# Attention with beacon keys and a two-layer MLP: pair 0's q by GpSimd's casting DMA, k first on SyncE's queue, four probability buffers

## The chip, the cores and the metric

The kernel runs on one core of one Trainium2 chip. The core has five engines with an instruction queue each: TensorE (PE, matmuls and transposes), ScalarE (ACT), VectorE (DVE), GpSimd (POOL) and SyncE (SP, which here only issues DMAs). Times are device microseconds of one execution; ten executions of the kernel before have a median of 351.33 us (350.22 to 353.68).

## The reference

For 8 batches and 8 heads, 576 queries of width 64 attend causally to 576 keys, and besides to 16 beacon keys that every query sees. The results of the heads are put side by side, and a two-layer MLP with a leaky ReLU follows on all 4608 rows.

```
k_all = concat([beacon_k, k]); v_all = concat([beacon_v, v])
a = softmax(where(causal, -1e9, q @ k_all.T / sqrt(64)))     # beacons never masked
x = (a @ v_all) -> rows (batch, query), columns (head, 64)   # 4608 x 512
h = x @ w_in                                                 # 512 x 2048
out = maximum(0.01 * h, h) @ w_out                           # 2048 x 512
```

## The kernel before

Work goes by *pairs* of heads, numbered g = 0 to 31: four pairs to a batch, two pairs to a *group* of `load_qk` (one load brings two pairs of one tensor, in two DMAs of q and two of k, one for each pair `e`). A matmul's 128 partitions hold the two heads of a pair.

For a pair, the steps are these. `t_q` transposes q (which = 0) or k (which = 1) on PE, 18 small transposes each into a PSUM tile `tp`, and DVE copies them in order into `qT` or into `kT`; from pair 8 on, a DMA transpose on SP (`turn_pairs`) and two GpSimd copies (`in_order`) do this instead. `beacon_columns` puts the 16 beacon keys into the first columns of `kT`. `score(g, n)`, n = 0 to 3, makes four blocks of transposed scores, and ACT takes the exponential of each block out of PSUM into the pair's probabilities `aT`. There are two PSUM buffers for scores, so block n + 2 waits for the exponential of block n. `masks_by_tri` (DVE, pairs 0 and 1) or `masks` (GpSimd, four instructions) clears what is above the diagonal. `value(g, 0)` and `value(g, 1)` multiply the probabilities with v, whose last column is one, so that the row sums come along; DVE takes the reciprocal and scales. `finish(g)` transposes the result on PE, and DVE copies it into `xT`, the MLP's operand.

The MLP goes in chunks of 512 rows. `fill()` issues the next *group* of four matmuls of 512 columns: `moe1` (first layer, followed by ACT's leaky ReLU) or `moe2` (a quarter of a second-layer tile). The first group needs `finish(3)`, that is all four pairs of batch 0, and the first half of `w_in`. These groups are the filling between the attention steps for the rest of the kernel.

Nothing is planned by a scheduler: `tc.manual_schedule` (L489) keeps each engine's instructions in the order in which the program writes them, and `tc` puts semaphore waits where data or buffers need them. The order by pairs is the loop of L573: pairs 0 to 4 in one branch (L577), pairs 5, 6 and 7 with a branch each, pair 8 and on in the general part. `keep_busy(n)` (L477) issues n small matmuls of the identity that compute nothing.

In the start (L499 to L522) the first pair goes its own way: `load_first_pair` (L141) loads q on SP and k on ACT in float32 into a borrowed `v_raw` tile, ACT and DVE cast them to bf16 (L510 to L512), and `t_q(0, 0)` and `t_q(0, 1)` follow on PE. All other q and k come by GpSimd's DMA, which casts on the way. `load_v(b, after)` issues v in six DMAs on SP, the first of which waits for another DMA. `cast_v` on GpSimd makes bf16 pieces of it. GpSimd's queue carries, in one order, its DMA issues, v casts, masks and beacon columns; a wait of one of them holds all that is behind it.

Buffers that matter: three `a_bufs` for probabilities (pair g has buffer g % 3, so pair 3's exponentials wait for value(0)), three `k_bufs`, three pairs of raw q and k tiles (`qkpool`), two PSUM buffers for scores and four (`ps_one`) for everything else.

## Time and profile before

| what | us |
|---|---|
| median of ten executions | 351.33 |
| the profiled execution | 350.98 |
| its span, first to last instruction | 349.3 |
| PE busy | 340.2 |
| ACT busy | 187.4 |
| POOL busy | 197.0 |
| DVE busy | 98.1 |
| PE's first scores start | 8.35 |
| first exponential starts | 8.78 |
| first MLP group starts | 28.75 |

Times within the span are counted from its first instruction. A line of the order of time shows start, duration, engine, source line, operation, tiles, shapes and how many instructions are merged in it; in square brackets stands how long the engine was idle before it, and what ended that. "SPq" and "POOLq" are the queues that issue DMAs. The share of a DMA queue is the time its packets took as a share of the core's 16 DMA engines; it can exceed 100%, as packets overlap.

### The profile page before, as it was taken

What the parts mean: (1) busy time and instruction counts of PE and PEld (TensorE: products, weight loads), DVE (VectorE), ACT (ScalarE), POOL (GpSimd) and SP (SyncE); (2) the same over time, 40 slices, a digit from 0 to 9 for tenths busy, and PEclk for the clock granted to TensorE, in tenths of its full rate; (3) what the DMA queues carried; (4) which work ended last, traced back from release to release, by engine and by line L of the source; (5) the groups of instructions that cost most, each with busy time, mean ns of one, the idle gap of its engine ahead of it and who ended that gap; (6) DMA issues with size and microseconds to landing.
All of it is one profiled execution on the core that took longest, in us unless ns stands there. A gap on an engine that the chain in (4) does not pass through costs nothing.

```text
span 349.3 us, 7405 instructions
## 1 busy us (share of the span) xinstructions
PE 340.2 (97%) x3045; PEld 172.8 (49%) x3045; DVE 98.1 (28%) x240; ACT 187.4 (54%) x277; POOL 197.0 (56%) x335
## 2 busy tenths in 40 slices
PE   8889999999999999999999999999999999999996
PEld 7564654334554444444544444455444554444444
DVE  3694530113342222222321223222321331000121
ACT  3987846665356863486347833684368304633300
POOL 7595837597999799767977779667321100000000
PEclk9999999999999999999999999999999999999999
DMA  8999999958969895992489319970110011000012
GB/s 163 193 157 202 176 212 180 201 111 164 236 147 135 158 151 108 186 191 49 82 181 186 88 34 190 185 124 31 52 41 0 2 76 46 0 30 32 30 60 92
DMA packets 85121, 40.88 MB, mean 117 GB/s; under 512 B 69040, under 2 KB 79280, under 8 KB 85088
## 3 DMA queue, kind: packets, MB, share of 16 engines
q1 hardware_dynamic: 72544, 26.52, 36.6%
q0 software_dynamic: 12128, 13.54, 24.9%
q10 hardware_dynamic: 416, 0.36, 0.5%
q8 instruction: 24, 0.39, 0.4%
q14 instruction: 9, 0.07, 0.1%
HBM read 37.22 MB, written 9.44 MB: 134 GB/s over the span
## 4 chain that ended last, share of the span: by engine, by line
PE 79%; DMA 11%; POOL 3%; SPq 3%; DVE 2%; issue 1%; ACT 0%; POOLq 0%
PE acc L444 36%; PE acc L422 28%; PE av L386 6%; PE sc L306 6%; DMA v_raw<-in_v_dram 4%; DMA q_raw<-in_q_dram 3%; SPq L218 2%; DMA q_turn<-q_nat 1%; DMA v_raw<-in_k_dram 1%; PE tp L408 1%; DVE osb L453 1%; DMA k_raw<-in_k_dram 1%; POOL aT L355 1%; DVE xT L413 1%; POOL v_aug L227 1%
## 5 line engine op out<-in xcount | busy, mean ns | idle before, releaser
L422 PE MATMUL acc<-xT,w_in_sb 128*128 128x512 bf16 x576 | 139.3, 379 | 1.4 <-DVE xT L413 1.4
L315 ACT ACTIVATE aT<-sc 128x1024 bf16<-128x1024 f32 (+3 forms) x128 | 103.8, 870 | 66.2 <-PE sc L306 60.7
L444 PE MATMUL acc<-w_out_sb,gT 128*128 128x512 bf16 (+1 forms) x592 | 139.0, 374 | 0.0
L429 ACT ACTIVATE gT<-acc 128x512 bf16<-128x512 f32 x144 | 85.7, 601 | 73.8 <-PE acc L422 73.6
L444 PEld LDWEIGHTS <-gT 128*128 128x128 bf16 x592 | 53.1, 98 | 58.5 <-issue 6.1
L422 PEld LDWEIGHTS <-w_in_sb 128*128 128x128 bf16 x576 | 51.8, 98 | 59.3 <-issue 4.6
L453 DVE COPY osb<-acc 128x512 f32<-128x512 f32 (+1 forms) x37 | 25.1, 677 | 127.8 <-PE acc L444 127.5
L355 POOL TENSOR_SCALAR_AFFINE_SELECT aT<-aT 128x224 bf16<-128x224 bf16 (+1 forms) x120 | 48.7, 447 | 18.7 <-PE av L386 9.9
L286 POOL COPY qT<-q_turn 128x576 bf16<-128x576 bf16 x24 | 28.6, 1194 | 40.0 <-PE sc L306 23.9
L386 PEld LDWEIGHTS <-aT 128*128 128x128 bf16 (+1 forms) x960 | 36.9, 98 | 15.6 <-issue 2.5
L386 PE MATMUL av<-v_aug,aT 128*128 128x65 bf16 (+1 forms) x960 | 40.1, 194 | 0.7 <-POOL v_aug L227 0.4
L306 PE MATMUL sc<-qT,kT 64*128 64x80 bf16 (+4 forms) x384 | 35.8, 283 | 2.4 <-ACT aT L315 1.5
L396 DVE TENSOR_TENSOR x_nat<-av,rec 128x384 bf16<-128x384 f32 x64 | 31.4, 491 | 2.2
L286 POOL COPY kT<-k_turn 128x576 bf16<-128x576 bf16 x24 | 28.5, 1186 | 0.8 <-DMA k_turn<-k_nat 0.8
L413 DVE COPY xT<-tp 128x576 bf16<-128x576 bf16 x32 | 14.5, 453 | 45.4 <-PE tp L408 45.4
L395 DVE RECIPROCAL rec<-av 128x6 f32<-128x6 f32 x64 | 11.9, 186 | 53.0 <-PE av L386 52.9
L306 PEld LDWEIGHTS <-kT 64*128 64x128 bf16 x384 | 12.3, 94 | 27.9 <-issue 16.2
L227 POOL CAST v_aug<-v_raw 128x512 bf16<-128x512 f32 (+1 forms) x35 | 20.8, 635 | 6.4 <-DMA v_raw<-in_v_dram 6.2
L133 POOL DMA_DIRECT2D q_raw<-in_q_dram x31 | 19.6, 632 | 4.5 <-DMA w_out_sb<-in_moe_w_out_dram 4.3
L133 POOL DMA_DIRECT2D k_raw<-in_k_dram x31 | 19.6, 633 | 3.5 <-DMA w_out_sb<-in_moe_w_out_dram 2.4
L408 PEld LDWEIGHTS <-x_nat 128*128 128x128 bf16 (+2 forms) x160 | 11.1, 97 | 6.7 <-DVE rec L395 0.2
L167 POOL COPY q_nat<-q_raw 128x1152 bf16<-128x1152 bf16 x12 | 13.9, 1156 | 0.3 <-DMA q_raw<-in_q_dram 0.3
(43 smaller groups left out, 94.3 us busy)
## 6 DMA issues: line engine op xcount, KB each, us to landing
out_dram<-osb SPq DMA_DIRECT2D x35, 256.0 KB, 2.4
v_raw<-in_v_dram SPq DMA_DIRECT2D x24, 256.0 KB, 5.0
q_raw<-in_q_dram POOLq DMA_DIRECT2D x31, 144.0 KB, 5.6
k_raw<-in_k_dram POOLq DMA_DIRECT2D x31, 144.0 KB, 6.1
w_in_sb<-in_moe_w_in_dram POOLq DMA_DIRECT2D x2, 1024.0 KB, 9.2
w_out_sb<-in_moe_w_out_dram POOLq DMA_DIRECT2D x2, 1024.0 KB, 12.4
v_raw<-in_v_dram SPq DMA_DIRECT2D x8, 224.0 KB, 3.8
v_raw<-in_v_dram SPq DMA_DIRECT2D x8, 160.0 KB, 4.4
```

The source lines that it names most:

```text
L133: dma = nc.gpsimd.dma_start(out=dst[e * RP : (e + 1) * RP], in_=src[b, h0 : h0 + 2].rearrange("h (p i) d -> p h i d", i=RI),)
L227: eng.tensor_copy(out=dst[0 : ROWS[c], c, :, 0:D], in_=t[0 : ROWS[c], c])
L286: nc.gpsimd.tensor_copy(out=dst.rearrange("c (p i) -> c p i", i=RI), in_=t[:, :, e].rearrange("c i p -> c p i"),)
L306: nc.tensor.matmul(out=sc[:, par, col - c0 : col - c0 + w], lhsT=kT[ps_, c * 128 : (c + 1) * 128], rhs=qT[ps_, q0 : q0 + w], start=True, s ...
L315: nc.scalar.activation(out=aT[:, :, c0 : c0 + w], in_=sc[:, :, 0:w], func=AF.Exp, scale=0.125)
L355: nc.gpsimd.affine_select(out=part, in_=part, compare_op=ALU.is_ge, fill=0.0, base=base, channel_multiplier=-1, pattern=pattern,)
L386: nc.tensor.matmul(out=avv[:, n, 0 : D + 1], lhsT=aT[0 : ROWS[c], par, a0 : a0 + 128], rhs=va[0 : ROWS[c], c, 2 * hp + par, :], start=(c = ...
L396: nc.vector.tensor_tensor(out=x_nat[:, t0:t1].rearrange("p t e d -> p (t e) d"), in0=avv[:, :, 0:D], in1=rec[:, n0:n1, None].to_broadcast( ...
L422: nc.tensor.matmul(out=acc, lhsT=w_in_sb[:, j, fc * 128 : (fc + 1) * 128], rhs=xT[:, j, i * 512 : (i + 1) * 512], start=(j == 0), stop=(j ...
L429: nc.scalar.activation(out=gT[i][:, fc, :], in_=acc, func=AF.Prelu, alpha=0.01)
L444: nc.tensor.matmul(out=acc[:, 0:w], lhsT=gT[i][:, fc, t * 128 : (t + 1) * 128], rhs=w_out_sb[:, fc, c0 : c0 + w], start=(fc == 0), stop=(f ...
L453: nc.vector.tensor_copy(out=osb[:, 0:w], in_=acc[:, 0:w])
```

## The change

Pair 0's q now comes by GpSimd's casting DMA straight to bf16 in its ordinary `q_raw` tile, issued right behind the identity and ahead of the other six q and k loads. k, still in float32, is the first DMA on SP's queue. Only k is cast, one head by ACT and one by DVE. k's transposes come before q's, and each of the two PSUM results is copied in halves by two engines (`copy_part`). The number of `keep_busy` matmuls before the first scores goes from 24 + 18 + 4 + 3 to 24 + 11 + 1 + 4. v(0) waits for pair 1's q.

There are four `a_bufs`, and two instead of three pairs of raw q and k tiles. The order of the early pairs is written anew: value(0,1) moves behind the third scores block of pair 3, value(1) and finish(0) into pair 3, value(2) and finish(1) into pair 4, value(3) and finish(2) into pair 5. In pair 5 the transposes for pair 6 come ahead of finish(3) and of the first MLP group. value(4) moves from pair 6 into pair 7, behind all scores of pair 7 and two MLP groups. Batch 1's four q and k loads of group 0 are issued together before v's second piece is cast, and `w_in`'s first half is issued before v's last two pieces are cast. In pair 7, `masks(7)` comes ahead of `load_qk(2, 0)`. Before pair 8's scores 31 instead of 30 MLP groups are done.

```diff
-    qkpool = ctx.enter_context(tc.tile_pool(name="qkpool", bufs=3))
+    qkpool = ctx.enter_context(tc.tile_pool(name="qkpool", bufs=2))
...
-    a_bufs = [singles.tile([128, 2, ACOLS], BF16, name=f"aT{i}") for i in range(3)]
+    a_bufs = [singles.tile([128, 2, ACOLS], BF16, name=f"aT{i}") for i in range(4)]
...
     def load_first_pair():
         load_beacon_k(0, 2, nc.scalar)
...
-        for eng, src, dst in zip((nc.sync, nc.scalar), (q, k), first_raw):
-            last = eng.dma_start(out=dst, in_=src[0, 0:2].rearrange("h (p i) d -> p h i d", i=RI))
-        return last
+        load_qk(0, 0, ())
+        q_rows, k_rows = qk_rows(0, 0, 0)
+        nc.sync.dma_start(out=first_k[0], in_=k_rows)
+        make_identity(nc, ident)
+        nc.gpsimd.dma_start(out=qk_raw[0, 0][0][0:RP], in_=q_rows)
...
-        parts = 2 if g == 0 and which == 1 else 1
-        for part in range(parts):
+
+        def copy_part(part, copy):
             p = slice(part * RP // parts, (part + 1) * RP // parts)
             copy(
...
+        return copy_part
+
+    def transpose_pair(g):
+        for which in range(2):
+            t_q(g, which)(0, nc.vector.tensor_copy)
...
-            probs[g] = a_bufs[g % 3]
+            probs[g] = a_bufs[g % 4]
...
-        first = load_first_pair()
-        make_identity(nc, ident)
-        load_qk(0, 0)
+        load_first_pair()
+        load_v(0, after=load_qk(0, 0, (1,))[0])
         load_qk(0, 1)
-        load_v(0, after=first)
...
         keep_busy(24)
         beacon_transposes(0, 2)
+        nc.scalar.copy(out=first_cast[:, 0], in_=first_k[0][:, 0])
+        nc.vector.tensor_copy(out=first_cast[:, 1], in_=first_k[0][:, 1])
         beacon_columns(0, nc.vector)
+        keep_busy(11)
+        copy_k = t_q(0, 1, 2)
+        copy_k(0, nc.scalar.copy)
+        keep_busy(1)
+        copy_q = t_q(0, 0, 2)
+        copy_q(0, nc.vector.tensor_copy)
+        copy_q(1, nc.scalar.copy)
+        copy_k(1, nc.vector.tensor_copy)
+        keep_busy(4)
         beacon_columns(1, nc.vector)
-        nc.vector.tensor_copy(out=first_cast[0], in_=first_raw[0])
-        nc.scalar.copy(out=first_cast[1][:, 0], in_=first_raw[1][:, 0])
-        nc.vector.tensor_copy(out=first_cast[1][:, 1], in_=first_raw[1][:, 1])
-        keep_busy(18)
-        t_q(0, 0)
-        keep_busy(4)
-        t_q(0, 1, nc.scalar.copy)
-        keep_busy(3)
...
-        cast_v(0, nc.gpsimd, 0, 1)
-        load_qk(1, 0, (0,))
...
             if g == 1:
+                cast_v(0, nc.gpsimd, 0, 1)
+                load_v(1, after=load_qk(1, 0)[-1])
                 beacon_columns(3, nc.gpsimd)
                 cast_v(0, nc.gpsimd, 1, 3)
-                load_v(1, after=load_qk(1, 0, (1,)))
+                load_w_in(0)
                 cast_v(0, nc.gpsimd, 3, 5)
-                load_w_in(0)
...
+            if g == 3:
+                score(3, 0)
+                score(3, 1)
+                transpose_pair(4)
+                score(3, 2)
+                value(0, 1)
+                score(3, 3)
+                masks(3)
+                value(1, 0)
+                value(1, 1)
+                finish(0)
+                continue
+
+            if g == 4:
+                score(4, 0)
+                score(4, 1)
+                transpose_pair(5)
+                value(2, 0)
+                score(4, 2)
+                value(2, 1)
+                finish(1)
+                score(4, 3)
+                masks(4)
+                continue
+
             if g == 5:
                 score(5, 0)
+                value(3, 0)
+                score(5, 1)
                 value(3, 1)
-                score(5, 1)
                 finish(2)
                 score(5, 2)
-                finish(3)
-                fill()
                 score(5, 3)
                 masks(5)
-                fill()
-                t_q(6, 0)
-                t_q(6, 1)
+                transpose_pair(6)
+                finish(3)
                 fill()
                 fill()
...
             if g == 7:
                 score(7, 0)
                 score(7, 1)
+                fill()
+                fill()
+                score(7, 2)
+                score(7, 3)
+                masks(7)
+                load_qk(2, 0)
+                value(4, 0)
+                value(4, 1)
                 value(5, 0)
                 finish(4)
                 value(5, 1)
-                score(7, 2)
-                score(7, 3)
-                load_qk(2, 0)
-                masks(7)
+                value(6, 0)
                 finish(5)
...
-                while done1[0] + done2[0] < 30:
+                while done1[0] + done2[0] < 31:
                     fill()
```

## The prediction

> **What bounds the kernel now.** I read the busy shares, then the stretches by stage, then TensorE's (PE's) waits, then the order of time.
>
> ```profile
> span 349.3 us, 7405 instructions
> PE 340.2 (97%) x3045; PEld 172.8 (49%) x3045; DVE 98.1 (28%) x240; ACT 187.4 (54%) x277; POOL 197.0 (56%) x335
> ```
>
> PE is busy 340.2 of 349.3 us, so at most 9.1 us can be had without removing matmuls, and nothing removes any but fillers. Stretches, cut at the first scores (8.35), at pair 3's scores (18.79), at the first MoE group (28.75) and at pair 8's scores; columns are width, PE, weight loads, DVE, ACT, POOL, clock, DMA share, GB/s:
>
> ```profile
> 0.00:8.35 8.35, 6.69 (x89) 6.04 (x89) 3.15 (x16) 2.82 (x5) 6.16 (x17) 1.00 0.83 161
> 8.35:18.79 10.44, 9.13 (x202) 6.01 (x203) 7.13 (x14) 9.64 (x13) 6.29 (x11) 1.00 1.14 192
> 18.79:28.75 9.96, 9.12 (x218) 6.67 (x215) 8.79 (x22) 8.07 (x10) 8.51 (x22) 1.00 1.00 164
> 28.75:66.00 37.25, 36.53 (x376) 18.91 (x374) 10.83 (x28) 24.54 (x40) 24.12 (x38) 1.00 1.14 191
> 66.00:346.00 280.00, 278.58 (x2172) 135.14 (x2169) 67.76 (x161) 142.36 (x212) 151.97 (x249) 1.00 0.52 102
> ```
>
> After 66 us PE loses 1.4 us in 280: the change touches nothing there but the number of probability buffers. Before 28.75 PE is not the bound. Up to 18.79 ACT's exponentials are (9.64 of 10.44; PE's time contains 28 filler matmuls); then DVE is nearly full (8.79 of 9.96). The same in ACT's and PE's order of time:
>
> ```profile
> 6.07 0.67 ACT L511 CAST k_nat<-v_raw 64x576 bf16<-64x576 f32 x1 [2.82 <-DMA v_raw<-in_k_dram]
> 7.38 0.47 PE L253 MATMUL tp<-ident,k_nat 64*64 64x64 bf16 x18
> 8.78 9.40 ACT L315 ACTIVATE aT<-sc 128x1024 bf16<-128x1024 f32 x12 [0.18 <-PE sc L306]
> 18.51 0.35 PE L386 MATMUL av<-v_aug,aT 80*128 80x65 bf16 x6 [0.43 <-POOL v_aug L227]
> 19.23 3.16 ACT L315 ACTIVATE aT<-sc 128x1024 bf16<-128x1024 f32 x4 [1.05 <-PE sc L306]
> 28.95 0.46 DVE L413 COPY xT<-tp 128x576 bf16<-128x576 bf16 x1 [0.19 <-PE tp L408]
> 30.96 0.47 PE L253 MATMUL tp<-ident,q_raw 64*64 64x64 bf16 x18
> ```
>
> Twelve exponentials run without a gap from 8.78 to 18.18 (3.13 per pair). Then ACT stands 1.05 us: pair 3's scores stand in PE's order behind all of value(0), because pair 3 reuses pair 0's buffer, and value(0,1) waited for the last piece of v. PE's waits over the run:
>
> ```profile
> PE sc L306 <- ACT aT L315: 1.5, 5, 0.5
> PE sc L306 <- POOL kT L286: 0.5, 1, 0.5
> PE av L386 <- POOL v_aug L227: 0.4, 1, 0.4
> ```
>
> **The change part by part.** (1) *Head.* Before: k, second on ACT's queue, lands at 6.03; casts to 6.74; its transposes at 7.38 behind pair 0's q transposes and four fillers; half copy; scores 8.35; first exponential 8.78. After: k is first on SP. Nearest row, q in that place: issued 0.81, landed 4.0 later, at 4.8. DVE is free at 4.9 (beacon copies at 4.43 + 0.46), casts end about 5.5 (0.67 ACT, 0.56 DVE). 24+2+11 fillers and beacon transposes end at 4.18 + 11 x 0.118 (18 took 2.13) = 5.48, so k's 18 transposes run 5.6 to 6.3 (0.69 as q's at 6.24, when matmuls were still slow). ACT's half copy 0.35 ends at 6.7; q's transposes 6.4 to 6.95; two half copies beside each other (0.40) 7.4; scores 7.45; plus 0.43 as before: first exponential 7.9, **-0.9**. It holds if q has landed by 6.4. q comes from GpSimd's casting queue, issued at 1.51. Rows:
>
> ```profile
> q_raw<-in_q_dram POOLq DMA_DIRECT2D x1, 144.0 KB, 5.2
> q_raw<-in_q_dram POOLq DMA_DIRECT2D x1, 144.0 KB, 3.5
> ```
>
> The first is that very slot (1.51 + 5.2 = 6.7), behind 640 KB of other queues; the second is the one at 15.53 on a calmer DMA (5.0). The Trainium skill ("DMA: Bandwidth & Descriptors", Latency and other measured facts) speaks against the move: first byte about 0.6 us on the hardware queues, about 1 us on GpSimd's. With SP's 4.0 us and 0.4 more, q lands at 5.9. After, only 352 KB stand before it; I take 5.7. By row two or the page it is hidden behind k's transposes; by row one the head gains 0.6 instead of 0.9. GpSimd has one DMA issue more (0.6 us) ahead of tri, which nobody needs before 14.
>
> (2) *v and the four casting loads.* v(0) now waits for pair 1's q (second GpSimd load, about 6.3) instead of k (6.03). That costs nothing, as v moved nothing before GpSimd's loads were through; here all traffic of 7.0 to 7.5, then of 14.5 to 15.0 (packets, MB, share):
>
> ```profile
> q0 software_dynamic: 99, 0.10, 122.6%
> ```
>
> ```profile
> q0 software_dynamic: 79, 0.09, 104.3%
> q1 hardware_dynamic: 39, 0.01, 9.3%
> ```
>
> The seven loads at 0.72 us each (0.1 MB per half us) from about 3.6 end at 8.7, where six ended at 9.2: v starts 0.4 earlier. But all four loads of batch 1's group 0 now stand together behind the cast of v's first piece (12), where before only two did, so v's last 0.2 MB waits for 2.9 instead of 1.4 us of them. The skill (same page, Queues, rings and completion order) says that an engine takes turns packet by packet, which is against this, as v's packets are 256 bytes: 900 of them against some 550 larger ones. The first row does not show turns at all, the second two to one. By turns the last piece lands near 17.3, by the row about 17.9 (before: 17.4). I take the row. GpSimd then: four issues to 14.5, two casts to 16.1-16.5, w_in issued at 16.1 to 16.9 (before 18.41), last cast (0.98) by 18.9.
>
> (3) *Fourth buffer, value(0,1) moved.* Pair 3's scores need no longer wait for value(0). Exponentials of pairs 0 to 2 end at 7.9 + 9.4 = 17.3; value(0,0) ends about 16.95 behind v's third piece; pair 3's exponentials start at 17.45 against 19.23: **-1.8**, of which 0.9 is the head. value(0,1) sits behind scores (3,2), at 18.75, just as its cast is done; stall 0 to 0.5, inside DVE's backlog.
>
> (4) *Pairs 3 to 5.* Now DVE sets the pace. Steps from the rows: two operand copies 1.36, a value 1.35, an xT copy 0.43. From value(0,1) at 19.45: its second half 0.65, value(1) 1.35, xT 0.45, copies for pair 5 1.4, value(2) 1.35, xT 0.45, value(3) 1.35, xT 0.45 ends at 26.9. Pair 6's copies follow from PE's transposes (26.85) to 28.6, and only then xT of pair 3, 29.05, which the first MoE group's fourth matmul needs. It ends at 29.4, before at 29.77. But scores (5,3) (0.2) and pair 6's transposes (0.68) are done by then, before not: 0.37 + 0.88 = **-1.25**. So 0.55 of the 1.8 is given back to DVE.
>
> (5) *Pair 6's operands.* Before they landed at 29.2 (q) and 30.1 (k), needed at 30.96. After they are needed at 26.85 to 27.2. GpSimd issues them about 20.5 (before 20.89), but they stand behind w_in in its queue: k landed 11.7 after w_in's issue. w_in 2.4 earlier gives 27.7: +0.1 beside DVE. Bounds: 26.5 (no cost) to 28.8 (+1.2).
>
> (6) *Later.* The waits of 40 to 45 us (0.24, scores of pair 7 in front of values) go, since MoE groups now stand there: -0.24. At pair 8, PE waited 0.48 for GpSimd's kT copy, the end of a chain w_in, w_out, beacons, q and k over GpSimd's queue. That chain starts from v(1), which follows the casting loads, and moves about 1.2 earlier; one group more (0.87) is put ahead of the scores, against PE's own lead of 1.4: -0.25 (0 to -0.48). The two qkpool buffers wait for transposes already done a pair earlier: nothing. Two more pad memsets run on DVE before 2 us, beside the loads. masks(7) ahead of load_qk(2,0) delays those issues some 1.6 us, but they stand behind w_out until 53.
>
> Sum: -1.25 + 0.1 - 0.24 - 0.25 = **-1.64**. The profiled execution took 350.98 (span 349.3 and 1.7 around it): 349.3. The median of ten is 351.33, 0.35 above it: **349.7**.
>
> **Rivals.** *All of the head's gain is kept* (DVE's copies slip into gaps, operands early): 1.9 + 0.24 + 0.48 = 2.6: 348.7. For it: ACT and PE alone would allow it; against it 8.79 of 9.96 us on DVE. *Late operands or late q*: pair 6's k at 28.8 (1.2 instead of 0.1), or q at 6.7 and pair 8's wait kept (0.3 + 0.25): 350.2 to 350.8, no change to speak of. For it: k landed only 0.86 before its use. *v's last piece is starved* by the four loads and w_in behind them: value(0,1) stops PE, with scores (3,3) and all of DVE's list behind it, and masks(2), then pair 6's loads, on GpSimd. Nothing is lost until the piece lands at 18.0; it turns to a loss at 18.0 + 1.64 = 19.6; if w_in (5.5 us) goes first it lands about 21, 3.0 late: 352.7. Against it: at 13.5 all but 0.23 MB had moved. *The change doesn't do what it says*: the head may not gain because q, not k, ends it; even then (3) and (6) remain.
>
> **How the numbers follow.** Likeliest 0.50 (own range 348.9 to 350.5), all kept 0.15, late operands 0.20, starved v 0.15. What this measurement can tell from no change is about 0.3%, 1.05 us: 350.28 to 352.38. Faster: 0.45 + 0.15 and a little of the third, 0.62; same 0.24; slower, most of the last, 0.14. Range 348.2 to 351.8: it takes in the best case and the late ones, and leaves out the worst of a starved v.
>
> **What would show it.** First exponential at 7.9 (7.5 to 8.3); pair 3's first at 17.45 with ACT's 1.05 us gone; v's last cast by 19; first MoE group ending near 29.4 with scores (5,3) behind it; a wait of PE on DVE's xT there; no wait on GpSimd's kT at 64. The prediction is wrong if v's last piece lands after 19.6, if pair 6's transposes wait over 1 us for their DMA, or if a new wait shows after 66.

## The result, and the profile after

The changed kernel has a median of 354.02 us (350.75 to 356.25, 14 executions); the kernel before, run beside it on the same chip, 351.57 us (49 executions). The ratio is 1.0054, with a 95% interval of 1.0033 to 1.0075: slower by 2.45 us in the medians. The forecast was 349.7 us in a range of 348.2 to 351.8. Both the range and the sign were wrong. An execution more than 1.5% above the fastest of its kernel, here the one of 356.25, is left out of the ratios and of the counts below.

The profiled execution took 353.82 us (span 352.1), 2.84 more than that of before, which had the full clock almost throughout (mean 0.999). Its busy shares and the row of TensorE's granted clock, from the page:

```profile
span 352.1 us, 7390 instructions
...
PE 341.3 (97%) x3036; PEld 173.1 (49%) x3036; DVE 99.8 (28%) x242; ACT 187.3 (53%) x277; POOL 197.0 (56%) x336
...
PEclk9969999999999999999999999999999999999999
```

The work is the same. New is the 6 in the last row: in the third of forty slices (17.6 to 26.4 us) the clock was well under full. The stretches, cut at the same events as before (first scores, pair 3's scores, first MLP group, pair 8's scores); columns are width, PE, weight loads, DVE, ACT, POOL, clock, DMA share, GB/s:

```profile
0.00:7.57 7.57, 5.04 (x79) 4.64 (x79) 2.84 (x18) 3.16 (x5) 5.91 (x18) 1.00 0.75 131
7.57:19.09 11.52, 9.03 (x186) 5.76 (x187) 7.11 (x12) 9.40 (x12) 5.24 (x9) 0.96 1.05 180
19.09:32.03 12.94, 12.76 (x273) 9.52 (x273) 9.58 (x24) 9.63 (x12) 9.51 (x24) 0.77 1.12 185
32.03:68.73 36.70, 35.66 (x335) 18.10 (x333) 9.99 (x27) 22.43 (x37) 25.61 (x40) 1.00 1.03 182
68.73:352.00 283.27, 278.81 (x2173) 135.10 (x2172) 70.25 (x162) 142.66 (x212) 150.72 (x246) 1.00 0.50 101
```

The first scores come 0.8 earlier than before (7.57 for 8.35). By pair 3's scores that lead has become a lag of 0.3 (19.09 for 18.79), by the first MLP group one of 3.3 (32.03 for 28.75). The third row says how: at a clock of 0.77 PE is busy 12.76 of 12.94 us, so for these 13 us PE itself is the bound; before, PE was busy 9.12 of 9.96 and DVE 8.79. Pair 8's scores come 3.6 later, of which 0.87 is the MLP group newly put ahead of them; what is left is the difference of the two executions. Nothing is lost after that. The order of time of ACT, GpSimd and PE:

```profile
4.83 0.67 ACT L512 CAST k_nat<-v_raw 64x576 bf16<-64x576 f32 x1 [1.62 <-DMA v_raw<-in_k_dram]
8.00 9.40 ACT L321 ACTIVATE aT<-sc 128x1024 bf16<-128x1024 f32 x12 [0.48 <-PE sc L312]
13.85 0.80 POOL L226 CAST v_aug<-v_raw 128x512 bf16<-128x512 f32 x1 [7.04 <-DMA v_raw<-in_v_dram]
17.08 1.58 POOL L226 CAST v_aug<-v_raw 128x512 bf16<-128x512 f32 x2
18.14 0.94 PE L392 MATMUL av<-v_aug,aT 128*128 128x65 bf16 x9 [1.49 <-POOL v_aug L226]
18.61 0.79 POOL L110 DMA_DIRECT2D w_in_sb<-in_moe_w_in_dram  x1
19.67 2.81 ACT L321 ACTIVATE aT<-sc 128x1024 bf16<-128x1024 f32 x3 [2.26 <-PE sc L312]
33.42 1.24 PE L428 MATMUL acc<-xT,w_in_sb 128*128 128x512 bf16 x5 [0.58 <-DVE xT L419]
```

GpSimd waits for v's first piece until 13.85. In the kernel before this line was

```profile
11.98 0.62 POOL L227 CAST v_aug<-v_raw 128x512 bf16<-128x512 f32 x1 [4.95 <-DMA v_raw<-in_v_dram]
```

Four DMA issues stand behind this cast, then the casts of pieces two and three at 17.08. value(0,0) on PE waits 1.49 us for them, and pair 3's scores stand behind value(0,0): ACT, which was to go on at 17.45, stands still for 2.26 us. PE's waits over the whole run:

```profile
PE acc L428 <- DVE xT L419: 2.0, 7, 0.6
...
PE av L392 <- POOL v_aug L226: 1.5, 1, 1.5
...
PE sc L312 <- ACT qT L259: 0.7, 1, 0.7
...
PEld L253 <- DMA q_raw<-in_q_dram: 0.8, 1, 0.8
```

The wait for GpSimd's kT at pair 8 is gone, as predicted. The waits alone don't account for what the stretches lost. The clock falls besides, here in steps of 1 us:

```profile
16.00:17.00 1.00, 0.50 (x7) 0.29 (x7) 1.00 (x3) 1.00 (x3) 1.00 (x3) 1.00 1.00 137
17.00:18.00 1.00, 0.00 (x0) 0.00 (x0) 1.00 (x2) 0.40 (x1) 1.00 (x2) 1.00 1.11 182
18.00:19.00 1.00, 0.72 (x9) 0.54 (x8) 0.19 (x1) 0.00 (x0) 1.00 (x3) 0.56 1.01 140
...
24.00:25.00 1.00, 1.00 (x20) 1.00 (x17) 0.76 (x3) 0.00 (x0) 1.00 (x3) 0.52 1.13 211
25.00:26.00 1.00, 1.00 (x29) 0.51 (x29) 0.81 (x3) 0.45 (x1) 1.00 (x3) 1.00 1.12 205
```

PE works 0.50 us in the two from 16 to 18. Then its clock falls to 0.50 and stays there for 7 us, although PE has work all the time.

### The profile page after: what moved, and what is told of

The parts are those of the page before. It is cut to its first block, busy times and chain, and to the rows that moved or that the text cites. A ratio compares the mean times of both kernels' runs of the same rounds, so it can differ in the third digit from the quotient of the medians.

```text
span 352.1 us, 7390 instructions
## 1 busy us (share of the span) xinstructions
PE 341.3 (97%) x3036; PEld 173.1 (49%) x3036; DVE 99.8 (28%) x242; ACT 187.3 (53%) x277; POOL 197.0 (56%) x336
## 4 chain that ended last, share of the span: by engine, by line
PE 90%; DVE 3%; DMA 3%; POOL 2%; issue 1%; ACT 1%; SPq 0%; POOLq 0%; ACTq 0%
PE acc L450 36%; PE acc L428 35%; PE av L392 8%; PE sc L312 8%; DMA v_raw<-in_v_dram 2%; PE tp L414 2%; DMA q_raw<-in_q_dram 1%; DVE osb L459 1%; DVE xT L419 1%; PE tp L253 1%; DVE x_nat L402 1%; ACT aT L321 1%; POOL v_aug L226 0%; POOL q_raw L135 0%; POOL k_raw L135 0%
## 5 line engine op out<-in xcount | busy, mean ns | idle before, releaser
L392 PEld LDWEIGHTS <-aT 128*128 128x128 bf16 (+1 forms) x960 | 37.8, 100 | 16.6 <-issue 4.3
L392 PE MATMUL av<-v_aug,aT 128*128 128x65 bf16 (+1 forms) x960 | 41.2, 197 | 1.6 <-POOL v_aug L226 1.5
L414 PE MATMUL tp<-ident,x_nat 128*128 128x128 bf16 (+2 forms) x160 | 14.0, 216 | 0.5 <-DVE x_nat L402 0.5
```

What stands on the lines that cost most here:

```text
L392: nc.tensor.matmul(out=avv[:, n, 0 : D + 1], lhsT=aT[0 : ROWS[c], par, a0 : a0 + 128], rhs=va[0 : ROWS[c], c, 2 * hp + par, :], start=(c = ...
L414: nc.tensor.transpose(ps[:, q0 : q0 + rows], x_nat[0:rows, t].rearrange("p e d -> p (e d)"), ident[0:rows, 0:rows],)
```

## The experiments

A number that every run gives beside its time is the mean granted clock. One stretch of 3.5 us at half clock lowers the mean over 350 us by 0.005, and the executions do fall on steps of about 0.005: 1.000 or 0.999, 0.995, 0.990, 0.985. "Full clock" below is a mean of at least 0.998. Of the 241 executions of the kernel before that stood beside the experiments, 147 had full clock (61%), with medians of 351.1 to 351.4 in the six sets of executions; the others had medians of 352.6 to 353.4. Over all six sets, losing the clock costs about 1.6 us in the median (352.8 for 351.2). Of the changed kernel 3 of 13 had it. The sets were run on five chips, so runs of different sets are compared by their ratios to the executions of the kernel before in the same set.

| run | median us | ratio to before (95%) | full clock | median of those |
|---|---|---|---|---|
| changed kernel | 354.02 | 1.0054 (1.0033 to 1.0075) | 3 of 13 | 353.2 |
| e1 start alone | 353.45 | 1.0041 (1.0020 to 1.0062) | 8 of 22 | 352.8 |
| e2 order alone | 352.35 | 1.0004 (0.9978 to 1.0030) | 5 of 14 | 351.2 |
| e3 fillers | 353.24 | 1.0054 (1.0032 to 1.0076) | 13 of 21 | 352.7 |
| e4 value(0,0) later | 354.54 | 1.0065 (1.0040 to 1.0091) | 0 of 14 | |
| f1 v behind k | 353.26 | 1.0045 (1.0023 to 1.0067) | 9 of 22 | 352.7 |
| f2 pair 3's loads later | 353.96 | 1.0058 (1.0036 to 1.0080) | 2 of 19 | 351.2 |
| f3 fillers, head too | 352.30 | 1.0024 (1.0003 to 1.0044) | 17 of 21 | 352.1 |
| g1 v behind k, fillers | 353.44 | 1.0031 (1.0012 to 1.0051) | 11 of 22 | 352.4 |
| g2 before, loads delayed | 351.56 | 0.9995 (0.9975 to 1.0015) | 10 of 14 | 351.1 |
| g3 before, fillers | 350.55 | 0.9962 (0.9948 to 0.9977) | 22 of 22 | 350.6 |
| h1 order, operands early | 352.28 | 1.0016 (0.9987 to 1.0045) | 6 of 14 | 351.2 |
| h2 the same, fillers | 352.48 | 1.0024 (1.0002 to 1.0045) | 12 of 21 | 351.6 |
| k1 before, seventh load | 351.33 | one execution | 1 of 1 | |
| k2 change, float32 twin | 356.16 | 1.0118 (1.0081 to 1.0155) | 0 of 4 | |
| k3 change, loads delayed | 356.52 | one execution | 0 of 1 | |
| l1 k1, timed | 352.72 | 1.0041 (1.0020 to 1.0063) | 6 of 20 | 352.0 |
| l2 k1 with fillers | 351.07 | 0.9990 (0.9961 to 1.0019) | 11 of 12 | 351.0 |

**Start or order (e1, e2).** e1 has the changed start (loads, copies, fillers of the first pair) in the kernel before, with its order, its three buffers of probabilities and its loads of batch 1 as they were:

```diff
-    a_bufs = [singles.tile([128, 2, ACOLS], BF16, name=f"aT{i}") for i in range(4)]
+    a_bufs = [singles.tile([128, 2, ACOLS], BF16, name=f"aT{i}") for i in range(3)]
...
+        cast_v(0, nc.gpsimd, 0, 1)
+        load_qk(1, 0, (0,))
...
-            if g < 3:
+            if g < 5:
...
```

> The changed start (k first on SP, q by GpSimd, copies by two engines, v behind pair 1's q) with the order, loads and buffers of the kernel before. Theory A (v's pieces land late because of the start: seven casting loads ahead of them): v's first piece is cast near 13.8 instead of 12.0, PE stops for it some 2 us in front of pair 3's scores, and the head's 0.8 is lost: 352 to 353.5, and the clock may drop. Rival B (the loss comes from the new order of loads and pairs 1 to 5): v is cast near 12.0 to 12.5, the head's 0.8 is kept: 350.5 to 351.

e2 is the other half: the start of before with the new order of pairs 3 to 7, the four buffers and the new loads. Against the changed kernel:

```diff
-        load_first_pair()
+        first = load_first_pair()
...
-        load_v(0, after=load_qk(0, 0, (1,))[0])
+        load_qk(0, 0)
...
+        load_v(0, after=first)
...
```

> The start of the kernel before with the new order, loads and buffers. Theory A (the start makes v late): v's first piece is cast near 12.0, the four casting loads put the second and third casts 1.2 us later than before (15.1 to 16.5), which is when value(0,0) needs them; no long stop, clock full: 349.5 to 351. Rival B (the order costs): PE stops at value(0,0) for over 1 us though the first piece is cast at 12, and the time is 352.5 to 354.

The loss follows the start: e1 loses 0.41%, e2 nothing that can be told. v's lateness follows the start in these two profiles, its first cast at 13.36 in e1 and at 11.45 in e2. In e1 PE stands 0.62 and 0.65 us within the head (waits for k's cast and for the last copy of q), as the changed kernel does. In this execution the clock fell at once. Its PE in order of time, and the stretch that follows:

```profile
5.54 0.48 PE L253 MATMUL tp<-ident,k_nat 64*64 64x64 bf16 x18 [0.62 <-ACT k_nat L512]
...
7.57 1.00 PE L312 MATMUL sc<-qT,kT 64*128 64x512 bf16 x4 [0.65 <-ACT qT L259]
```

```profile
8.00:10.00 2.00, 2.00 (x43) 1.28 (x39) 0.77 (x2) 1.78 (x2) 0.00 (x0) 0.50 1.19 213
```

Four score matmuls take 1.00 us instead of 0.59, and half clock lasts from 7.5 to 18. e2 does early on what the order was forecast to do: sixteen exponentials without a gap. In its profile PE later stands still at pair 6's operands:

```profile
8.64 12.50 ACT L315 ACTIVATE aT<-sc 128x1024 bf16<-128x1024 f32 x16 [0.18 <-PE sc L306]
...
28.84 0.47 PE L253 MATMUL tp<-ident,q_raw 64*64 64x64 bf16 x18 [1.25 <-DMA q_raw<-in_q_dram]
29.86 0.47 PE L253 MATMUL tp<-ident,k_raw 64*64 64x64 bf16 x18 [0.55 <-DMA k_raw<-in_k_dram]
```

After these waits half clock lasts from 30.5 to 34.5.

**The clock (e3, f3, g3; e4).** Fillers compute nothing and go where PE would stand. e3 puts 24 ahead of value(0,0):

```diff
+                    keep_busy(24)
                     value(0, 0)
```

> The changed kernel with 24 filler matmuls in front of value(0,0), where PE waited 1.5 us for v. They add no useful work and v comes no earlier. Theory C (the half clock from about 18 to 25 us is set off by PE standing still there, and costs time): the clock stays full over 18 to 26, the values of pairs 0 and 1 run at 0.56 instead of 1.0 per half, and the time falls by 1 to 3 us, to 351 to 353. Rival D (the half clock comes by itself, or lies on time that DVE and ACT hide): clock as in the changed kernel, or the time the same within 0.5: 353.5 to 354.5.

f3 has them in the head as well:

```diff
-        keep_busy(4)
+        keep_busy(10)
         beacon_columns(1, nc.vector)
...
+                    keep_busy(24)
                     value(0, 0)
```

> The changed kernel with 24 fillers ahead of value(0,0) and 10 instead of 4 ahead of the first scores, where PE stood still 0.65 us. Theory C (standing still in the start or at value(0,0) makes the clock go to half in many executions): executions with full clock become as frequent as in the kernel before (6 of 10) or more, where the changed kernel has 3 of 13; the median falls by about 1 us, to 353. v stays late, so the executions with full clock stay 1 to 1.5 us above those of the kernel before. Rival D (the clock's drops come by themselves): the share of full-clock executions stays at 2 to 4 of 10.

Executions at full clock go from 3 of 13 to 13 of 21 and 17 of 21. In f3 the loss is less than half of the change's (1.0024 for 1.0054, though the intervals overlap); in e3 it is as large as before the fillers (1.0054), with the clock full as often as in the kernel before. So the fillers restore the clock, and not by that alone the time. Part of that is their own price: in e3's profile the 24 keep PE until 17.75, where v's second piece had been cast by 16.5. Pair 3's exponentials come 1 us earlier than in the changed kernel:

```profile
18.64 3.16 ACT L321 ACTIVATE aT<-sc 128x1024 bf16<-128x1024 f32 x4 [1.23 <-PE sc L312]
```

But v came 1 us earlier too in that execution, at 12.86, and the execution is the fastest of e3's 22 (350.94). In f3's profile v is not late at all:

```profile
11.93 0.62 POOL L226 CAST v_aug<-v_raw 128x512 bf16<-128x512 f32 x1 [5.13 <-DMA v_raw<-in_v_dram]
```

The changed kernel, e1, e3, e4 and f3 have the same loads up to this cast, and it starts at 13.85, 13.36, 12.86, 13.81 and 11.93; in the six profiles with the start of before and six casting loads (before, e2, g2, g3, h1, h2) at 11.45 to 12.30. v is later with the changed start as a rule, but by an amount that differs from execution to execution. g3 asks whether the same holds in the kernel before, where no step of the change is present:

```diff
                 if g < 2:
                     keep_busy(3)
...
+                if g == 2:
+                    keep_busy(8)
                 score(g, 3)
                 if g < 2:
-                    keep_busy(4)
+                    keep_busy(6)
                 if g == 2:
                     value(g - 2, 0)
+                    keep_busy(6)
```

> The kernel before with 18 more fillers where PE stood still in front of pair 2's last scores and between the halves of value(0), and behind the scores of pairs 0 and 1. They do no useful work. Theory C (stillness of PE in the first 25 us sets off the half clock, in the kernel before too): executions with full clock rise from 0.65 to 0.8 or more, the median falls by 0.2 to 0.5 us. If stillness there has nothing to do with it: share as before, median the same or up to 0.5 higher.

It does: all 22 executions at full clock, and 350.55 us, faster than the kernel before (0.9962, 0.9948 to 0.9977), which had full clock in 26 of 51 beside it. Its page:

```profile
span 348.7 us, 7397 instructions
...
PEclk9999999999999999999999999999999999999999
```

e4 tries another cure for the gap and fails. It lets pair 3's first two scores pass ahead of value(0,0):

```diff
-                    value(0, 0)
...
                 score(3, 0)
                 score(3, 1)
+                value(0, 0)
```

> The changed kernel with value(0,0) behind the first two score blocks of pair 3, which the fourth buffer allows. Theory A/C (PE and ACT stop because value(0,0) with its late v stands in front of pair 3's scores): pair 3's exponentials follow pair 2's without the gap of 2.26, PE stands still 0.9 less, and the time falls 1 to 2.5 us, to 351.5 to 353. Rival E (pair 4's q and k, landed only at 19.9, or DVE bound this stage anyway): the gap moves to pair 4's transposes and the time stays within 0.7 of the changed kernel's.

ACT's gap ahead of pair 3 is gone, but no execution of 14 has full clock and the time is 354.54. In its profile half clock comes early, from about 8.7 to 12.3, behind a wait of 0.7 us in the head. An earlier exponential alone brought nothing; why no execution kept the clock is not shown.

**When v comes (f1, f2, g1, g2).** f1 lets v wait for SP's k, not for the second casting load:

```diff
-        load_v(0, after=load_qk(0, 0, (1,))[0])
+        load_qk(0, 0, (1,))
+        load_v(0, after=k_dma)
```

> The changed kernel with v(0) waiting for k on SP (landed at 4.8) instead of pair 1's q (6.5 to 6.9), all else as changed. Theory A1 (v is late because its issue waits for a load of the casting queue, and so stands behind all seven casting loads): v's issue moves to about 4.9, ahead of the last loads, its first piece is cast by 12 instead of 13.8, and the time at full clock falls by 1 to 2 us. Theory A2 (v is late because the seven casting loads themselves run slower, 0.15 instead of 0.20 MB/us, from their early start on): the first cast stays within 0.6 of 13, the time within 0.7 of the changed kernel's.

v is issued at 4.73 instead of 6.66. Its first cast is at 12.44, which lies within the 11.93 to 13.85 of the same loads without this edit. The ratio is 1.0045 for 1.0054, no difference that these runs can tell. From 7.5 to 8.5 us v's packets (q1) move beside those of the casting queue (q0):

```profile
q0 software_dynamic: 143, 0.15, 98.6%
q1 hardware_dynamic: 103, 0.02, 13.0%
```

f2 takes pair 3's two loads out of v's way:

```diff
-        load_qk(0, 1)
+        load_qk(0, 1, (0,))
...
         beacon_columns(2, nc.gpsimd)
+        load_qk(0, 1, (1,))
```

> The changed kernel with the two casting loads of pair 3 issued behind tri and the ones (about 6.5) instead of at 4.6 and 5.2, so that five instead of seven stand ahead of v's issue at 6.7. Pair 3's operands are needed at 14.6. Theory A2 (what stands ahead of v in the DMA engines makes it late): 1.4 us less stands there, v's first piece is cast at 12 to 12.6, the second and third by 16.5, PE's stop at value(0,0) falls from 1.5 to under 0.5, and the time at full clock falls by 1 us or more. Rival (the engines take turns by packet, so that the two loads delay v wherever they are issued): first cast as before at 13 to 13.8, no gain.

First cast at 12.74, and a new wait of 1.6 us for pair 4's k, with half clock from 18.5 to 26: nothing gained. g1 puts f1 and ten fillers at each of f3's places together:

```diff
-        keep_busy(4)
+        keep_busy(10)
...
+                    keep_busy(10)
                     value(0, 0)
```

> The changed kernel with v(0) waiting for k, 10 instead of 4 fillers ahead of the first scores and 10 ahead of value(0,0): both causes treated. If v's late issue and PE's stillness are the causes, the share of executions with full clock is 7 of 10 or more and these have a median of 350.5 to 351.5, so that the whole is 350.8 to 352 and no slower than the kernel before. If something else in the start or the order costs (a slower casting stream, pair 6's operands), full-clock executions stay at 352 or above.

It was to be no slower than the kernel before and was (353.44, 1.0031). v's first cast is at 12.66, and its PE waits 1.0 and 0.4 us for pair 6's operands, as in e2. g2 delays the casting loads of the kernel before, by making tri and the ones first:

```diff
         make_identity(nc, ident)
+        make_tri()
+        make_ones()
         load_qk(0, 0)
```

> The kernel before with tri and the ones ahead of its six casting loads, so that these are issued from about 2.8 to 6.4 instead of 1.5 to 5.2, and are still being issued when the stream starts to move at 4.6. Theory O (the casting stream is slower while GpSimd still issues loads, as it does in the changed start): it moves 0.30 instead of 0.40 MB in 5 to 7 us, v's first piece is cast at 12.6 or later instead of 12.0. Rival (what slows it is the seventh load or the mix with k on SP): 0.36 to 0.40 MB in 5 to 7, first cast within 0.6 of 12.0.

The casting stream has 0.35 MB between 5 and 7 us for 0.40 in the kernel before, v's first cast stays at 11.97, and so does the time (351.56). From 6 us on the stream moves its 0.19 MB in each us as before. So following close on the issues is not what makes the changed start slow.

**Pair 6's operands (h1, h2).** h1 is e2 with pair 6's q and k issued ahead of `w_in`, and both behind pair 3's transposes:

```diff
-                load_w_in(0)
-                cast_v(0, nc.gpsimd, 3, 5)
...
-                load_qk(1, 1, (0,))
...
+                if g == 2:
+                    load_qk(1, 1, (0,))
+                    load_w_in(0)
+                    cast_v(0, nc.gpsimd, 3, 5)
```

> The start of the kernel before with the new order (as e2), and pair 6's q and k issued ahead of w_in's first half instead of four microseconds behind it; w_in and v's last two casts follow behind them. Theory F (the new order saves PE's time, and loses it again waiting 1.25 + 0.55 us for pair 6's operands behind w_in, which also sets off a half-clock stretch at 30): these waits are gone, pair 6's transposes run near 27.5, executions with full clock take 349.5 to 350.3 instead of 351.1, and full clock is more frequent than 5 of 14. Rival G (w_in, now 1.4 us later, is itself needed at 28, so that the wait goes to the first MLP group): a wait of 1 us or more for w_in's DMA, full-clock executions at 350.7 to 351.3.

h2 has 18 fillers besides, as many as g3 and nearly in the same places:

```diff
+                if g == 2:
+                    keep_busy(8)
...
-                    keep_busy(4)
+                    keep_busy(6)
...
+                    keep_busy(6)
```

> As h1, with the 18 fillers of g3 in front of pair 2's last scores, behind the scores of pairs 0 and 1 and ahead of value(0,0). Theory C and F together: nearly all executions at full clock, median 349.5 to 350.3, below the kernel before with fillers (350.55). If the late w_in or DVE takes the order's gain, the median is 350.5 to 351.3, no better than fillers alone.

The waits for pair 6 are gone, and yet 352.28 and 352.48. In both profiles PE stands within value(3,1), with no wait that the profile can name. h1:

```profile
27.75 0.61 PE L386 MATMUL av<-v_aug,aT 128*128 128x65 bf16 x12 [1.66 <-issue]
```

Half clock follows, from 28 to 35. What held PE stays open. A packet of the instruction queue q14 moved inside the stall in both (26.75 to 27.00 in h1, 27.50 to 27.75 in h2), which would fit late instructions; but k2 has a stall of 1.5 us of this kind at about 30 us, and no such packet between 29 and 32.

**What slows the casting stream (k1, k2, k3, l1, l2).** Packets of GpSimd's casting queue from 5 to 7 us (packets, MB, share), in the kernel before and then in the changed kernel:

```profile
q0 software_dynamic: 380, 0.40, 119.3%
```

```profile
q0 software_dynamic: 292, 0.30, 104.9%
```

The order is not the reason: with the start of before, five profiles of other kernels have 0.35 to 0.40 MB there (0.35 is g2); with the changed start the profiles of e1, e3, e4, f1, f2, f3 and g1 have 0.27 to 0.33. k1 is the kernel before with one casting load more, a second copy of pair 0's q at the head of the queue, which nothing uses:

```diff
             if b == 0 and grp == 0 and e == 0:
+                nc.gpsimd.dma_start(
+                    out=qk_raw[b, grp][0][0:RP], in_=q[b, h0 : h0 + 2].rearrange("h (p i) d -> p h i d", i=RI)
+                )
                 continue
```

> The kernel before with pair 0's q loaded a second time, by a casting load at the head of GpSimd's queue, so that seven casting loads stand there as after the change; nothing uses the extra copy. Its first pair still comes in float32 by SP and ACT. Theory N (the seventh load at the head is what slows the stream): 0.28 to 0.33 MB of casting packets from 5 to 7 us and v's first cast at 13 or later. Theory B (the stream is fast when it starts behind k's float32 transfer on ACT's queue, which the change took away): 0.38 to 0.40 MB as before, and v's first cast later only by one load, about 12.4 to 12.7.

k2 is the changed kernel with a second copy of q in float32 on ACT's queue, where k used to stand:

```diff
+        twin = t[0:RP].rearrange("p c h d -> p (c h d)")[:, 2 * RI * D : 4 * RI * D]
+        nc.scalar.dma_start(out=twin.rearrange("p (h i d) -> p h i d", h=2, i=RI), in_=q_rows)
         nc.sync.dma_start(out=first_k[0], in_=k_rows)
```

> The changed kernel with pair 0's q loaded a second time in float32 on ACT's queue, where k stood before the change; nothing uses the extra copy. Theory B: the casting stream then moves 0.38 to 0.40 MB from 5 to 7 us, although there is more to move; pair 0's q lands later than 5.5, at 6.5 or so, and the first exponential comes at 8.5 to 9; v's first cast near 12.5. Theory N: 0.27 to 0.33 MB as in the changed kernel, and v's first cast at 13.5 or later. The time by theory B 352 to 353, by theory N 354 or more.

k3 makes tri and the ones between pair 0's q and the other six loads:

```diff
         load_first_pair()
+        make_tri()
+        make_ones()
         load_v(0, after=load_qk(0, 0, (1,))[0])
```

> The changed kernel with tri and the ones of v made between pair 0's q and the other six casting loads, so that these are issued some 1.3 us later. Theory T (the stream is slow where its packets follow close on their issue, and fast where issues have run ahead): the six move at 0.14 to 0.17 MB in each us at first, since they are again moved as they are issued, and 5 to 7 us shows 0.27 to 0.33 MB; theory N as well. If the gap lets SP's k finish first and that is what counts (theory B in another form), 0.36 MB or more from 6 to 8 us.

In k2 the stream is back at its old rate, in the same two microseconds:

```profile
q0 software_dynamic: 364, 0.38, 118.3%
```

After 6 us it moves 0.19 to 0.21 MB in each. k1 is less plain. Its 5 to 7 us are within what theory N had said, as is its first cast at 13.03; the same kernel profiled again (l1) has what theory B had said, with a first cast at 12.36:

```profile
q0 software_dynamic: 318, 0.33, 101.7%
```

```profile
q0 software_dynamic: 373, 0.39, 117.0%
```

What separates all profiles is the next stretch. From 6 to 7 us the ten with a float32 transfer on ACT's queue (k1 with its 0.14 from 5 to 6 among them) move 0.19 or 0.20 MB, the nine without it 0.14 to 0.17. k2, which adds the transfer alone, changes sides. So the transfer on ACT's queue goes with the rate, whether six or seven loads follow; that this is because packets gather behind it is only argued. After 7 us the nine differ among themselves: k3 stays at 0.15 to 0.17, e1, e3, e4 and f3 reach 0.19.

The rate is not all of v's lateness. The last casting packet moves at 10.8 in k2 and 10.6 in l1, no earlier than in the changed kernel (10.5), which begins its stream a microsecond sooner; yet their first casts come at 12.55 and 12.36, not at 13.85. k2 is no remedy. Its q lands late, the first exponential starts at 9.06 and half clock lasts from 7.5 to 18.5: 356.16 us, where 352 to 353 had been expected.

k3 is slow without a long wait for v. In its one execution PE waits only 0.35 us for v and fifteen exponentials run without a gap. Then pair 6's q is late. Its ACT and PE in order of time, and two stretches:

```profile
8.13 12.05 ACT L321 ACTIVATE aT<-sc 128x1024 bf16<-128x1024 f32 x15 [0.48 <-PE sc L312]
...
29.82 0.69 PE L253 MATMUL tp<-ident,q_raw 64*64 64x64 bf16 x18 [1.89 <-DMA q_raw<-in_q_dram]
```

```profile
28.00:30.00 2.00, 0.18 (x7) 0.18 (x9) 0.00 (x0) 0.96 (x2) 0.98 (x3) 0.92 1.27 196
30.00:32.00 2.00, 1.85 (x42) 1.53 (x39) 1.37 (x2) 0.00 (x0) 0.85 (x3) 0.50 1.40 169
```

l1 times k1's kernel, and l2 adds g3's fillers to it:

> The kernel before with the seventh casting load again, now timed. v's first cast comes about 1 us late in it (13.0 instead of 12.0) and PE stops 0.9 us at value(0,0). Theory L (a late v costs by itself, also where the clock stays full): the executions with full clock have a median of 352.3 or more, as in the kernel with the changed start and the order of before (352.8). Theory S (in the order of before the lateness is absorbed by the work behind it; only PE's standing still costs, through the clock): those with full clock 351.1 to 351.6, fewer of them than six in ten, and a median of 351.8 to 352.8.

> The same with the fillers that gave the kernel before 350.55 (keep_busy(8) ahead of pair 2's last scores block, 6 instead of 4 in pairs 0 and 1, 6 between value(0,0) and value(0,1)). Theory S: nearly all executions at full clock, 350.5 to 351.1. Theory L: nearly all at full clock too, but 351.7 or more.

One more casting load ahead of v, and nothing else, costs as much as the whole changed start: 1.0041, like e1. The one execution of k1 shows that it need not: its PE stops 0.86 us at value(0,0), the clock stays full, and it takes 351.33. In l1's profile v's first cast is at 12.36, PE stands 0.23 and 0.60 us inside value(0), and the clock goes:

```profile
17.94 0.44 PE L389 MATMUL av<-v_aug,aT 128*128 128x65 bf16 x9 [0.23 <-POOL v_aug L230]
18.98 0.45 PE L389 MATMUL av<-v_aug,aT 80*128 80x65 bf16 x6 [0.60 <-POOL v_aug L230]
```

```profile
20.00:22.00 2.00, 2.00 (x50) 1.65 (x48) 1.09 (x3) 1.86 (x2) 2.00 (x6) 0.50 0.78 73
```

With fillers (l2) 11 of 12 executions have full clock, and the loss is gone (0.9990). Neither theory is wholly right. The late v seems to have a price of its own: l1's six executions at full clock have 352.0 where before has 351.1, and l2 has 0.9990 where g3 has 0.9962, though these intervals overlap. About half of l1's loss goes with the clock, by the working at the end of the next section.

## Why the prediction was wrong

**(1) The head: right.** First exponential at 8.00 (forecast 7.9, before 8.78). q by GpSimd's casting queue landed 4.0 us after its issue, just as k did on SP, so the 0.4 us added for GpSimd's slower first byte, after the Trainium skill ("DMA: Bandwidth & Descriptors"), did not show in the landing. It shows in part in the first packets: k's moved at 2.3, 1.5 us after its issue, q's at 3.3, 1.8 after. What the sum did not weigh is that the new head has fewer fillers and lets PE stand 0.45 and 0.65 us.

**(2) v and the casting loads: the step that failed.** "Seven loads at 0.72 us each end at 8.7" took the rate of 0.20 MB in a us from the kernel before. That rate belonged to a stream standing behind k's float32 transfer on ACT's queue (k2), which the change takes away. At 0.14 to 0.17 the last of the seven's packets moved at 10.5; the six of before had theirs at 9.9. So v's turn came 0.6 later, where the step had it 0.4 earlier. That is a third of v's lateness: it had its first cast at 13.85, not 12. The other 1.3 us lie behind the stream. From its last packet to the first cast pass 3.35 us here, 3.1 and 3.3 in e1 and e4, but 2.0 and 2.2 in f3 and e3 with the same loads, and 2.1 before. From 13 to 14 us v's queue moves only 0.07 MB, with no other queue beside it. The step took this part as unchanged; what lengthens it stays open. `w_in` then had its issue at 18.61, not 16.1 to 16.9, and the last cast ended at 20.57, not 18.9. The choice that v's packets take no turns with the casting queue was read from stretches in which v had hardly begun: in f1 they do move side by side.

**(3) Pair 3's exponentials: fell with (2).** 19.67 instead of 17.45. The fourth buffer does what it is for: in e2, with v on time, sixteen exponentials run without a gap. But value(0,0) still stands ahead of pair 3's scores, and v's second and third piece, not the last one, which I had watched, were late for it.

**(4) DVE as the bound: not reached.** The fourth matmul of the first MLP group waited 0.58 us for DVE's xT, as forecast, but at 33.4 instead of 29. Between 18 and 25 the bound was PE at half clock. "Before 28.75 PE is not the bound" was also a weak reading of its line, in which PE is busier than DVE (9.12 for 8.79 of 9.96).

**(5) Pair 6's operands: mis-sized.** The sum had +0.1, with q and k at 27.7 and an upper bound of 28.8. In e2 PE waits 1.25 and 0.55 us until 28.84 and 29.86, in k3 1.89 until 29.82. In the changed kernel it doesn't show, since PE is late itself. So a cure of (2) alone would probably not have brought the gain: in the profiles of g1, k3, h1 and h2 PE stands still again between 26 and 30 us.

**(6) Later: right.** No wait for kT at pair 8, and none of PE over 0.3 us after 36.

**The clock: left out.** The sum took PE's durations at full clock throughout, and had no term for losing it. That PE standing still brings its loss is shown by g3, e3 and f3. How much of the loss it makes is an estimate. At the same step of the mean clock the changed kernel's executions are still 0.9 to 2.0 us above those of before in the median (353.2 for 351.2 at full clock, 353.3 for 352.4 at 0.995, 354.0 for 352.8 at 0.99, 354.8 for 353.8 below, with three or four executions at each). The means of before at these four steps, weighted with the changed kernel's shares, give 352.6; the mean of before itself is 351.9 and that of the changed kernel 353.7. So about 0.7 of 1.9 us in the mean come from the rarer full clock and about 1.2 from what is slower besides; in l1 the same working gives 0.6 of 1.2. f3, which gives the clock back to 17 of 21 executions, keeps 0.8 of 1.9 us by the ratios; e3, with 13 of 21, keeps all. The split is not settled.

The rival "v's last piece is starved" named the right place, value(0) in front of pair 3's scores, but the wrong piece, and 352.7. That a lead of 0.8 us at the head did not survive is shown. What e1's executions at full clock lose (352.8 for 351.2) is not shown in any profile, as e1's profiled execution was at half clock for 10 us; it stays open.

## What to carry to other kernels

Look at PE's longest nearly empty stretch before counting microseconds: on this kernel, whose PE is 97% busy, executions that lost the clock took 1.6 us more, and a few matmuls of nothing where PE would stand were the best cure found (350.55 for 351.87 in the kernel before). A transfer rate read from a profile belongs to the queues that ran beside it, and can change when one of them is taken away. Look at more than one execution before taking the landing of a DMA as fixed: with the same loads v's first cast came anywhere from 11.93 to 13.85. Before pulling a chain forward, list when each later operand lands: the next late one takes the gain back.

## What the runs showed of the hardware

*When the clock falls.* In the 19 profiles, I took the emptiest 2 us of PE between 5 and 37 us. In eight kernels (the changed one, e2, f2, g1, h1, h2, k2, k3) PE was busy 0.18 to 0.79 us in them, and half clock followed within 3 us in all eight. With 0.91 to 1.37 us busy it followed in some (e1, l1) and not in others (before, g2, k1, e3, f1, l2); in e4 it had come and gone earlier, behind 1.35 us busy from 6 to 8. With 1.4 and more (f3, g3) it did not come. The Trainium skill ("TensorE: Matmul & The Clock Gate", Part 1) has the clock halved after at least one idle window of about 3.4 us, and full again after at least one busy window. The half rate agrees (0.50), and so does the return. The fall does not: PE was never empty for 3.4 us in this stretch, the longest wait before a fall in the changed kernel was 1.49 us, and where half clock was over before the profile's 37 us it mostly lasted 7 us, in two cases about 4 and in two 10 to 11. If an idle window has to be an empty one, none of these executions would have lost the clock. Its free-running window of that length may be seen in the steps of 3.5 us, and would explain why the same program keeps the clock in one execution and loses it in another; that is argued, not shown.

*Two queues side by side.* In the changed kernel v's DMAs were issued on SP from 6.66 on, and not one packet of that queue moved between 7 and 9 us, while GpSimd's casting queue moved 0.34 MB. That is not a queue held back to the end: the first came at 9.0, 2.4 us after the issue, and from 9 to 10 us 306 packets of v moved beside 144 of the casting queue. k, in the quiet start, needed 1.5 us from issue to first packet, so of the 2.4 us only about 0.9 (an estimate) are due to the traffic.
